# Attention, gated MLP and a spectral block on one core: row maxima for two heads at a time, more score buffers, one load for w_sg, a last product in fp16 halves, and the remaining tokens in two column groups

## The chip, the cores and the metric

The kernel runs on one core of a Trainium2 chip. The metric is the device time of one launch in microseconds (us), the median of several runs. A core has TensorE (PE in the profile, its weight loads PEld), VectorE (DVE), ScalarE (ACT), GpSimd (POOL) and SyncE (SP), which here only issues DMAs; ACT issues some as well. Each engine works through its own list of instructions in order, and waits on semaphores for the others.

## What is computed

Three blocks on a batch of 4 with 576 tokens, in float32; the outputs of one are the input of the next.

```python
def _attn_ref(q, k, v, w1, b1, w2):            # 4 batches, 8 heads, 576 tokens, 64 wide
    scores = scale * np.matmul(q, k.transpose(0, 1, 3, 2))
    ...
    h = np.maximum(x @ w1 + b1, 0.0)           # x: one number for each pair of positions
    bias = h @ w2
    scores = scores + bias.transpose(2, 0, 1)[None, :, :, :]
    scores = scores - np.max(scores, axis=-1, keepdims=True)
    attn = np.exp(scores)
    attn = attn / (np.sum(attn, axis=-1, keepdims=True) + 1e-09)
    return np.matmul(attn, v)

def _moe_ref(x, w_in, g_ln, w_sg, b_sg, w_out):
    h = gelu(x @ w_in)                         # tanh form
    u, v = (h[..., :512], h[..., 512:])
    v_n = (v - mu) / np.sqrt(var + 1e-06) * g_ln
    v_s = np.einsum('ts,bsd->btd', w_sg, v_n) + b_sg[None, :, None]
    return x + (u * v_s) @ w_out

def _moe2_ref(x, w_theta, w_tok_r, w_tok_i, w_ch):
    theta = x @ w_theta
    y = np.einsum('ts,bsd->btd', w_tok_r, x * cos(theta)) + np.einsum('ts,bsd->btd', w_tok_i, x * sin(theta))
    u = x + y
    return u + np.maximum(u @ w_ch, 0.0)
```

## The kernel before

**Tiling.** The 576 tokens are four tiles of 128 and one of 64. Heads go in pairs p (0 to 3) of a batch. Most products use fp16 halves: a float32 tile is scaled by a power of two and split into a high half and the rest, and three products (high·high, high·rest, rest·high) replace one. The final product with w_ch (`cp`) and that with w_out (`op`) split float32 into two tiles of TensorE's rounded float32 type instead.

**Order.** All operations are first recorded. A planner (`plan`, L433) then writes each engine's list, from a key of each operation, the tables `BIAS` and `SHIFT` (numbers for each group and for each kind of tile on each engine) and estimated costs (`cost`, L600). It also chooses the engine where the code offers several: a load may go to SP's or ACT's queue. Every instruction is emitted by one line, L417, so the profile's rows are told apart by the names of the tiles.

**Stages of the profiled execution.** To 80 us the bias of all heads is generated (tiles `pb`, `hq`, `bs`). From 80 to 190 us batch 0's attention runs, with w_in and w_sg being loaded and converted (`w1_load`, L806; raw tiles `rawwi`, `ws`). From 190 to 510 us attention of batches 1 to 3 runs mixed with the MLP of the batch before. From 510 to 650 us come batch 3's MLP, the products with w_out (`op`), conversion of the second block's weights, and the scales of its inputs. From 650 us on it is theta (`tp`), the token mix (`yp`) and the last product (`cp`).

**Attention.** `scores` (L865) fills PSUM tiles `s`, two heads at a time (128 tokens by 576). `att_tile` (L884) handles one head's tile: on DVE one pass adds the bias, writes `e`, and reduces the row's minimum into `m`; one more instruction adds a constant to the column `m`; ACT takes the exponential of `e` in place; ACT copies the high half into `p`, POOL subtracts for the low half; SP's queue issues a transposing DMA `pT`<-`p`; 14 matmuls `px` follow. Buffers: 3 of `e`, 4 of `m`, 6 of `p`, 7 of `pT`. The fifth token tile packs two heads' 64 rows (`pair_rem`, L920).

**The MLP.** `v_unit` (L1007) computes `vp`, x times the v half of w_in, for a token tile t: 12 matmuls of 512 columns out; then gelu, mean and variance (`st`, `mv`), the normalising factor (`nk`), and the two halves `n`, or `nr` for t = 4, where only 64 of the 128 partitions are used. `s_unit` (L1049) is the product with w_sg. Results pass through DRAM (`dg`, `dx`).

**The second block.** `conv_w` (L1142) loads and converts a weight tile, `put_w` (L1154) writes its two halves. `scale_of` (L1171) sums squares over partitions and makes a power of two by seven one-column instructions (`fs`, `fa`, `fb`, `fc`). `x_scale` (L1220) does so for each batch's input. `s4` (L1300) splits u into `sp_u` and computes `cp`; for each of four column blocks of a batch DVE takes the maximum with zero and adds u in one instruction (`bias<-cp,bias`: the output tile lies in old bias storage), and a DMA stores it.

## Time and profile before

| | |
|---|---|
| median of 3 runs | 831.53 us (829.93 to 832.4) |
| the profiled execution's own time | 833.19 us |
| its span, first to last instruction | 831.4 us |
| PE, share of the span busy | 88% (728.1 us) |
| PEld | 56% (465.0 us) |
| DVE | 73% (607.9 us) |
| ACT | 61% (507.0 us) |
| POOL | 41% (343.6 us) |
| DMA packets | 120.78 MB, mean 145 GB/s |
| mean granted TensorE clock | 0.926 |

The shares are means over stages with different limits, so the table of busy time by stretch is read first, then the chain of waits in each stretch (the chain goes back from the last instruction, at each step to what released it), and then single groups of instructions. In a row of groups the numbers behind x are the count, the busy time, the mean of one in ns, and the engine's idle time just before them with who ended it.

### The profile page before, as it was taken

What the parts mean: (1) busy time and instruction counts of PE and PEld (TensorE: products, weight loads), DVE (VectorE), ACT (ScalarE), POOL (GpSimd) and SP (SyncE); (2) the same over time, 40 slices, a digit from 0 to 9 for tenths busy, and PEclk for the clock granted to TensorE, in tenths of its full rate; (3) what the DMA queues carried; (4) which work ended last, traced back from release to release, by engine and by line L of the source; (5) the groups of instructions that cost most, each with busy time, mean ns of one, the idle gap of its engine ahead of it and who ended that gap; (6) DMA issues with size and microseconds to landing.
All of it is one profiled execution on the core that took longest, in us unless ns stands there. A gap on an engine that the chain in (4) does not pass through costs nothing.

```text
span 831.4 us, 17445 instructions
## 1 busy us (share of the span) xinstructions
PE 728.1 (88%) x6490; PEld 465.0 (56%) x6490; DVE 607.9 (73%) x1453; ACT 507.0 (61%) x953; POOL 343.6 (41%) x274
## 2 busy tenths in 40 slices
PE   5787368579889998989889988999889999999998
PEld 2233235256455554644545545776656677677887
DVE  6896388887887587975997989898988844572422
ACT  6896477666787676867747774565466642560500
POOL 0011334434666664756615662354246541360400
PEclk9998657578999998999978999999999999999999
DMA  6777959789998999889789777554452221030101
GB/s 196 193 181 155 261 133 216 166 160 190 188 188 191 169 205 182 160 180 213 195 212 199 157 157 203 172 157 164 117 120 54 40 53 56 1 80 29 44 15 58
DMA packets 221429, 120.78 MB, mean 145 GB/s; under 512 B 195360, under 2 KB 195744, under 8 KB 221344
## 3 DMA queue, kind: packets, MB, share of 16 engines
q1 hardware_dynamic: 211936, 98.86, 55.5%
q10 hardware_dynamic: 9408, 20.81, 7.9%
q8 instruction: 51, 0.84, 0.4%
q14 instruction: 34, 0.28, 0.1%
HBM read 47.68 MB, written 14.16 MB: 74 GB/s over the span
## 4 chain that ended last, share of the span: by engine, by line
PE 38%; DVE 15%; DMA 6%; issue 6%; ACT 3%; POOL 2%; ACTq 0%; DVEq 0%; POOLq 0%; SPq 0%
PE yp L417 11%; PE cp L417 6%; PE s L417 5%; DMA pT<-p 5%; PE sp L417 4%; PE px L417 3%; PE tp L417 3%; DVE bias L417 3%; PE up L417 3%; PE vp L417 2%; DVE e L417 2%; PE op L417 1%; DVE biasr L417 1%; DVE sp_g L417 1%; DVE gg L417 1%
## 5 line engine op out<-in xcount | busy, mean ns | idle before, releaser
L417 POOL TENSOR_TENSOR p<-e,p 128x576 f16<-128x576 f32 x144 | 190.3, 1332 | 240.8 <-ACT p L417 213.4
L417 PE MATMUL s<-kq 64*128 64x288 f32 (+1 forms) x640 | 153.3, 482 | 34.0 <-DVE m L417 32.3
L417 ACT ACTIVATE e<-e,m 128x576 f32<-128x576 f32 x144 | 110.5, 767 | 71.8 <-DVE m L417 51.9
L417 PEld LDWEIGHTS <-pT 128*128 128x128 f16 (+1 forms) x2240 | 84.2, 108 | 69.2 <-DMA pT<-p 32.5
L417 DVE CUSTOM_DVE_ANT_0 e<-s,bias 128x576 f32<-128x576 f32 x128 | 95.5, 750 | 35.8 <-PE s L417 29.9
L417 PE MATMUL px<-v,pT 128*128 128x64 f16 (+1 forms) x2240 | 95.5, 203 | 23.3 <-DMA pT<-p 19.2
L417 PEld LDWEIGHTS s<-kq 64*128 64x128 f32 (+1 forms) x640 | 70.5, 194 | 80.5 <-DVE m L417 46.7
L417 ACT ACTIVATE p<-e 128x576 f16<-128x576 f32 x144 | 94.7, 673 | 8.2 <-DMA pT<-p 3.3
L417 PEld LDWEIGHTS <-z 128*128 128x128 f16 x864 | 84.1, 98 | 25.5 <-ACT z L417 2.3
L417 PE MATMUL yp<-bias,z 128*128 128x288 f16 x576 | 76.5, 286 | 1.6 <-ACT z L417 1.6
L417 PE MATMUL pb<-hq,w2s 128*32 128x288 f32 x576 | 52.8, 430 | 17.1 <-ACT bs L417 8.1
L417 PE MATMUL op<-sp_g,wo 128*128 128x288 f32 x384 | 58.1, 307 | 7.6 <-ACT sp_g L417 2.8
L417 PE MATMUL vp<-wi,xT 128*128 128x512 f16 (+1 forms) x240 | 63.1, 400 | 0.7 <-DVE gg L417 0.5
L417 PEld LDWEIGHTS op<-sp_g,wo 128*128 128x128 f32 x384 | 53.6, 194 | 13.0 <-ACT sp_g L417 3.8
L417 PE MATMUL up<-xT,wi 128*128 128x64 f16 (+1 forms) x384 | 57.8, 290 | 0.0
L417 PE MATMUL sp<-ws,n 128*128 128x64 f16 (+1 forms) x384 | 56.9, 286 | 0.9 <-DVE gtu L417 0.7
L417 PE MATMUL cp<-sp_u,wc 128*128 128x288 f32 x384 | 54.0, 300 | 0.2 <-DVE bias L417 0.2
L417 PEld LDWEIGHTS cp<-sp_u,wc 128*128 128x128 f32 x384 | 51.8, 188 | 1.2 <-DVE bias L417 0.4
L417 DVE TENSOR_SCALAR hq<-lt,nl 128x576 f32<-128x576 f32 x96 | 45.7, 544 | 4.2 <-PE pb L417 2.3
L417 PEld LDWEIGHTS pb<-hq,w2s 128*32 128x32 f32 x576 | 20.8, 112 | 47.4 <-ACT bs L417 17.9
L417 PE MATMUL tp<-wt,xh 128*128 128x512 f16 x192 | 44.7, 380 | 1.9 <-DVE xh L417 1.9
L417 DVE SCALAR_TENSOR_TENSOR bias<-yp,iy,bias 128x576 f32<-128x576 f32 x16 | 13.0, 814 | 41.6 <-PE yp L417 41.5
(222 smaller groups left out, 1222.2 us busy)
## 6 DMA issues: line engine op xcount, KB each, us to landing
bias<-bs SPq DMA_DIRECT2D x32, 288.0 KB
kq<-kq SPq DMA_DIRECT2D x10, 576.0 KB
gr<-dg SPq DMA_DIRECT2D x15, 288.0 KB
out<-bias SPq DMA_DIRECT2D x15, 288.0 KB
xx<-dx SPq DMA_DIRECT2D x14, 288.0 KB
raw<-vp ACTq DMA_DIRECT2D x11, 320.0 KB
kq<-kq ACTq DMA_DIRECT2D x6, 576.0 KB
bias<-w_tok SPq DMA_DIRECT2D x6, 576.0 KB
```

Source lines behind the costliest of these rows:

```text
L417: getattr(getattr(self.nc, name), m)(*[res(x) for x in a], **out)
```

## The change

Six things are changed.

1. **Maxima of two heads.** A new `att_max` makes `e` for both heads of a token tile, with both minima in one two-column tile, and adds the constant once for both. `m` goes from 4 one-head buffers to 2 two-head ones, `e` from 3 buffers to 5, `p` from 6 to 5 and `pT` from 7 to 6.
2. **w_sg in one transfer**, where there were five.
3. **The remaining 64 tokens of `v_unit`**: each matmul of 64 rows by 512 becomes two of 64 by 256, into partitions 0 to 63 and 64 to 127, so that what follows works on 128 partitions by 256. Small copies move statistics between the partition halves, and `nr` is put together by two casts, a copy and two subtractions.
4. **The last product in scaled fp16 halves.** `wc` and the halves of u (`uh` instead of `sp_u`) are fp16, with power-of-two scales. w_ch's squares are summed in addition (four more ACT instructions), the scale of u comes from a bound, by the new `pow_of`. ACT now evicts `cp` with Relu and the inverse scale, and a DVE addition of u follows.
5. **Scales share one tile** `small`, of which each is a column.
6. **The planner**: the cost of 64-row outputs is halved, `SLACK` of ACT's loads is 0.456 instead of 0.038, and all numbers of `BIAS` and `SHIFT` are others.

```diff
 SHIFT = {
-    "@a0": 41.9784, "@a1": 58.4206, "@a10": -87.1642, "@a11": -56.0582, "@a12": -234.3945, "@a13": -112.4685,
...
+    "@a0": -222.2232, "@a1": 118.0225, "@a10": -218.6815, "@a11": 63.2763, "@a12": -170.5693, "@a13": -132.864,
...
+        late = U(SLACK if e == 2 else QUEUE) if op.dma and op.cost[i] > 0 else 0
...
-            self.ld(self.wsl[st], d["w_sg"][:, st])
+        self.ld(self.wsg[:, :5], d["w_sg"])
...
+    def att_max(self, b, p, t, tiles):
...
+        m = a.tile([P, 2, n], F32, tag=f"m{n}", bufs=2, name=f"m{b}_{p}_{t}")
...
+            s = a.tile([P, S], F32, tag="s", bufs=5, name=f"e{b}_{p}_{t}_{e}")
+            nc.vector.tensor_tensor_reduce(out=s.rearrange("p (n j) -> p n j", n=2), in0=ps[:, :, :SH],
+                                           in1=bias.rearrange("p (n j) -> p n j", n=2),
+                                           scale=-0.125, scalar=3e38, op0=ALU.add, op1=ALU.min,
+                                           accum_out=m[:, 0, e:e + 1])
...
+        nc.vector.tensor_scalar(m[:, 1], m[:, 0], LN2E, None, op0=ALU.add)
...
-        p16 = a.tile([P, 2, S], F16, tag="p16", bufs=6, name=f"p{u}")
+        p16 = a.tile([P, 2, S], F16, tag="p16", bufs=5, name=f"p{u}")
...
-        pT = a.tile([P, 9, P], F16, tag="pT", bufs=7, name=f"pT{u}")
+        pT = a.tile([P, 9, P], F16, tag="pT", bufs=6, name=f"pT{u}")
...
-                nc.tensor.matmul(ps[:m], self.xt_tok(b, cc, s, t), self.wi[:, w, cc, 512:DFF],
-                                 start=(cc == 0 and i == 0), stop=(cc == 3 and i == 2))
+                for h in range(P // m):
+                    nc.tensor.matmul(ps[h * m:h * m + m, :n], self.xt_tok(b, cc, s, t),
+                                     self.wi[:, w, cc, 512 + h * n:512 + h * n + n],
+                                     start=(cc == 0 and i == 0), stop=(cc == 3 and i == 2))
...
+        nc.vector.tensor_tensor(t, t, self.ck, op=ALU.mult)
+        u, w = self.pow_of(t, f"u{b}")
+        self.su[b] = u, w
...
-        sp = self.x_prep(b, self.p_sp2, "u", key - 10)
+            self.split16(x, self.x1[b][:, f], su)
...
+        nc.vector.tensor_tensor(ic, iu, self.ic, op=ALU.mult)
...
-            nc.vector.scalar_tensor_tensor(o.rearrange("p (n t) -> p n t", n=2), ps[:, :, :SH], 0.0,
-                                           self.x1[b][:, db].rearrange("p (n t) -> p n t", n=2),
-                                           op0=ALU.max, op1=ALU.add)
+            nc.scalar.activation(o.rearrange("p (n t) -> p n t", n=2), ps[:, :, :SH], AF.Relu, scale=ic)
+            self.tt(("vector", "gpsimd"), o, o, self.x1[b][:, db], ALU.add)
...
-        self.wc = self.p_s2.tile([P, 2, 4, DM], F32R, tag="wo", name="wc")
+        self.wc = self.p_s2.tile([P, 2, 4, DM], F16, name="wc")
+        sc, self.ic, _ = self.scale_of(self.ssq["w_ch"], "c")
```

The order is shown at three places. The first is ACT's list in batch 0's attention, where w_in's first two raw tiles are loaded; `p_0_1_2` stands for pair 0, head 1, token tile 2 (in `e_0_3_1` of the kernel after: pair 0, tile 3, head 1). Before:

```order
L417 ACTIVATE p_0_1_2_103<-e_0_1_2_1028 128x576
L417 DMA raw_1_1190<-vp 128x640
L417 DMA rawwi_0_1136<-w_in 128x1024
L417 DMA rawwi_1_1137<-w_in 128x1024
L417 ACTIVATE e_0_0_3_1107,sm_0_104<-e_0_0_3_1107,m_0_0_3_928 128x576
L417 ACTIVATE e_0_1_3_1144,sm_0_104<-e_0_1_3_1144,m_0_1_3_1080 128x576
L417 ACTIVATE p_0_0_3_791<-e_0_0_3_1107 128x576
L417 ACTIVATE p_0_1_3_925<-e_0_1_3_1144 128x576
L417 ACTIVATE v_1_114<-raw_1_1190,fc_v_207 128x2x320
```

After:

```order
L417 ACTIVATE p_0_0_3_728<-e_0_3_0_715 128x576
L417 ACTIVATE p_0_1_3_831<-e_0_3_1_809 128x576
L417 DMA raw_1_1174<-vp 128x640
L417 DMA rawwi_0_1130<-w_in 128x1024
L417 DMA rawwi_1_1131<-w_in 128x1024
L417 DMA ws<-w_sg 128x2880
L417 ACTIVATE e_0_4_0_878,sr_0_2_85<-e_0_4_0_878,m_0_4_87 128x576
L417 ACTIVATE e_1_4_0_1088,sr_1_2_86<-e_1_4_0_1088,m_1_4_88 128x576
L417 ACTIVATE p_0_2_0_902<-e_0_4_0_878 128x576
```

The loads of `rawwi` now stand behind the copies of `p` for token tile 3, and w_sg's single load has joined them on this list.

The second is SP's list at the start of batch 3's attention; here the first digit of a `pT` is the batch, then pair, head and tile, and `bias0<-w_out` and `bias0<-w_tok` are loads of raw weights for the second block. Before:

```order
L417 DMA bias0_78<-w_out 128x1024
L417 DMA dg_58<-gg1_2_5504 128x512
L417 DMA dx_57<-xT2_1_3939 128x1152
L417 DMA bias0_78<-w_tok 128x1152
L417 DMA dg_58<-gg1_3_5646 128x512
L417 DMA_TRANSPOSE pT3_0_1_2_5767<-p3_0_1_2_5433 128x9x128
L417 DMA dx_57<-xT2_2_5610 128x1152
L417 DMA bias0_78<-w_tok 128x1152
L417 DMA dx_57<-xT2_3_5614 128x1152
L417 DMA kq3_3_5883<-kq 128x1152
L417 DMA raw3_1_5932<-vp 128x640
L417 DMA_TRANSPOSE pT3_0_0_3_5962<-p3_0_0_3_5483 128x9x128
```

After:

```order
L417 DMA bias0_78<-w_out 128x1024
L417 DMA bias0_78<-w_tok 128x1152
L417 DMA dx_57<-xT2_1_3862 128x1152
L417 DMA_TRANSPOSE pT3_0_0_2_5630<-p3_0_0_2_5331 128x9x128
L417 DMA dx_57<-xT2_2_5549 128x1152
L417 DMA dg_58<-gg1_4_5637 512x1x64
L417 DMA dx_57<-xT2_3_5553 128x1152
L417 DMA bias0_78<-w_out 128x1024
L417 DMA kq3_3_5784<-kq 128x1152
L417 DMA raw3_1_5813<-vp 128x640
L417 DMA bias0_78<-w_tok 128x1152
L417 DMA_TRANSPOSE pT3_0_1_2_5842<-p3_0_1_2_5360 128x9x128
```

Before, ten loads stand around the transpose `pT3_0_1_2`, three of them raw weights. After, ten stand around `pT3_0_0_2` in these rows, four of them raw weights, and three more loads (one `bias0<-w_tok`, two `dg`) stand ahead of the first row, behind the transpose of `p3_0_1_1`: thirteen in all, five of raw weights, before `pT3_0_1_2` is issued.

The third is the end of the program. DVE's last rows before (`bias_78<-cp_0,bias_75` is maximum and sum of one column block):

```order
L417 SCALAR_TENSOR_TENSOR bias_75<-yp_2_10214,iy_123,bias_75 128x576
L417 TENSOR_TENSOR sp_u_10203<-bias_75,sp_u_10203 128x576
L417 SCALAR_TENSOR_TENSOR bias_75<-yp_3_10273,iy_123,bias_75 128x576
L417 TENSOR_TENSOR sp_u_10211<-bias_75,sp_u_10211 128x576
L417 SCALAR_TENSOR_TENSOR bias_78<-cp_0_10331,bias_75 128x576
L417 SCALAR_TENSOR_TENSOR bias_78<-cp_1_10389,bias_75 128x576
L417 SCALAR_TENSOR_TENSOR bias_78<-cp_2_10418,bias_75 128x576
L417 SCALAR_TENSOR_TENSOR bias_78<-cp_3_10444,bias_75 128x576
```

DVE after:

```order
L417 SCALAR_TENSOR_TENSOR bias_75<-yp_1_10173,small,bias_75 128x576
L417 SCALAR_TENSOR_TENSOR uh_3_10100<-bias_75,small,uh_3_10100 128x576
L417 SCALAR_TENSOR_TENSOR bias_75<-yp_2_10174,small,bias_75 128x576
L417 SCALAR_TENSOR_TENSOR uh_3_10163<-bias_75,small,uh_3_10163 128x576
L417 SCALAR_TENSOR_TENSOR bias_75<-yp_3_10236,small,bias_75 128x576
L417 SCALAR_TENSOR_TENSOR uh_3_10171<-bias_75,small,uh_3_10171 128x576
L417 TENSOR_TENSOR bias_78<-bias_78,bias_75 128x576 x4
```

ACT's last rows after, each `bias_78<-cp` being one eviction:

```order
L417 ACTIVATE uh_3_10091<-bias_75,small 128x576
L417 ACTIVATE uh_3_10100<-bias_75,small 128x576
L417 ACTIVATE uh_3_10163<-bias_75,small 128x576
L417 ACTIVATE uh_3_10171<-bias_75,small 128x576
L417 ACTIVATE bias_78<-cp_0_10294,small 128x576
L417 ACTIVATE bias_78<-cp_1_10352,small 128x576
L417 ACTIVATE bias_78<-cp_2_10383,small 128x576
L417 ACTIVATE bias_78<-cp_3_10408,small 128x576
```

The four evictions have gone from DVE to ACT, and DVE adds u to each behind them.

## Rows read from the trace of the kernel before

**Rows 1.** the page's chain of waits: share of the span by engine.

```profile
PE 38%; DVE 15%; DMA 6%; issue 6%; ACT 3%; POOL 2%; ACTq 0%; DVEq 0%; POOLq 0%; SPq 0%
```

**Rows 2.** busy time by stretch (columns in the first row), from batch 0's attention to the end.

```profile
core 0: us, PE busy (x) PEld busy (x) DVE busy (x) ACT busy (x) POOL busy (x), PEclk, DMA share, GB/s
80.00:190.00 110.00, 72.58 (x584) 43.70 (x580) 82.20 (x227) 73.54 (x156) 43.35 (x32) 0.62 0.82 184
190.00:300.00 110.00, 104.01 (x1144) 60.06 (x1143) 84.88 (x258) 82.50 (x168) 68.04 (x57) 0.99 0.95 187
...
405.00:510.00 105.00, 92.93 (x1035) 53.41 (x1034) 92.81 (x247) 66.86 (x132) 51.37 (x42) 0.90 0.83 189
510.00:650.00 140.00, 125.51 (x820) 87.26 (x819) 123.81 (x229) 81.98 (x149) 60.10 (x45) 0.99 0.47 133
650.00:831.40 181.40, 176.85 (x1315) 141.90 (x1312) 80.95 (x98) 64.49 (x103) 52.76 (x41) 1.00 0.13 39
```

**Rows 3.** chain from 650 us: its shares, then pieces (start, length, what).

```profile
by line: PE yp L417 50.4%; PE cp L417 28.1%; PE tp L417 11.9%; POOL z L417 2.0%; issue 1.5%; DVE bias L417 1.3%; DVE rr L417 1.2%; ACT rk L417 0.7%; DVE xh L417 0.4%; ACT xh L417 0.4%; ACT rr L417 0.4%; ACT z L417 0.4%; POOLq L417 0.0%
...
794.99 19.86 PE yp L417 x162
814.86 12.80 PE cp L417 x96
```

**Rows 4.** TensorE matmuls by shape (count, busy us, mean ns; idle before).

```profile
L417 PE MATMUL cp<-sp_u,wc 128*128 128x288 f32 x384 | 54.0, 300 | 0.2 <-DVE bias L417 0.2
```

**Rows 5.** timeline of the last 20 us (start, length, engine, operation).

```profile
815.74 0.69 ACT L417 ACTIVATE sp_u<-bias 128x576 fp32r<-128x576 f32 x1 [5.93 <-DVE bias L417]
...
827.68 0.76 DVE L417 SCALAR_TENSOR_TENSOR bias<-cp,bias 128x576 f32<-128x576 f32 x1 [2.44 <-PE cp L417]
```

**Rows 6.** ScalarE and VectorE groups by shape.

```profile
L417 ACT ACTIVATE bs<-pb,cb,rp 128x576 f32<-128x576 f32 x13 | 10.7, 823 | 3.9 <-DMA bias<-bs 2.3 <-PE pb L417 1.6
...
L417 DVE TENSOR_SCALAR m<-m 128x1 f32<-128x1 f32 x144 | 20.6, 146 | 1.1
...
L417 DVE TENSOR_TENSOR wc<-bias,wc 128x512 fp32r<-128x512 f32 x4 | 4.5, 1162 | 0.5 <-ACT wc L417 0.5
```

**Rows 7.** timeline of 86 to 98 us, ScalarE and its queue.

```profile
88.39 7.25 ACTq L417 DMA_DIRECT2D rawwi<-w_in  x2
...
95.75 0.77 ACT L417 ACTIVATE e<-e,m 128x576 f32<-128x576 f32 x1 [9.06 <-DMA rawwi<-w_in]
```

**Rows 8.** timeline pieces of TensorE: 64 columns wide, and bias generation's 32 columns.

```profile
12.37 2.15 PE L417 MATMUL pb<-hq,w2s 128*32 128x288 f32 x32
...
274.07 0.97 PE L417 MATMUL px<-v,pT 128*64 128x64 f16 x28
...
457.12 2.13 PE L417 MATMUL vp<-wi,xT 128*64 128x512 f16 x9
```

**Rows 9.** waits: who waited for whom (us in total, times, longest).

```profile
DVE e L417 <- POOL p L417: 7.2, 8, 1.9
```

**Rows 10.** SyncE's queue at batch 3's start.

```profile
396.80 4.08 SPq L417 DMA_TRANSPOSE pT<-p  x2
402.03 0.46 SPq L417 DMA_DIRECT2D bias<-w_out  x1
...
408.87 2.04 SPq L417 DMA_TRANSPOSE pT<-p  x1
411.31 0.32 SPq L417 DMA_DIRECT2D dx<-xT  x1
...
428.68 11.04 SPq L417 DMA_TRANSPOSE pT<-p  x6
```

**Rows 11.** chain in the same stretch.

```profile
417.17 16.56 issue
433.73 6.24 DMA pT<-p
```

**Rows 12.** VectorE's one-column arithmetic in a scale's chain.

```profile
L417 DVE TENSOR_SCALAR fa_x<-fa_x x8: 141/153/153, 579.3 to 644.5; 128x1 int32<-128x1 int32 x8
```

More of the change, by code (lines that the diff above doesn't have):

```diff
@@ L290 @@
-    "z": -223.7223, "zb": 1431.7686,
-}
-LOADF, LOADK = 9.424364169007852, 9.769672874286008e-139
-BV = -1.2289825808293022
[5 rows of a table added]
+    "@w_ch": 826.9009, "@w_out": 1276.3767, "@w_theta": -275.07, "@w_tok": 690.6464, "@y0": -945.0649,
[3 rows of a table added]
+    "fa_wi": 241.9602, "fa_ws": 866.725, "fac": -197.6344, "fb_v": 1268.1131, "fb_wi": -171.3458,
+    "fb_ws": -1066.8603, "fc_v": 939.5478, "fc_wi": -1431.7327, "fc_ws": 1172.4657, "fd_v": -453.2562,
+    "fd_wi": -530.3092, "fd_ws": 430.504, "fs": 0.2305, "fs_v": 808.5659, "fs_wi": 1806.8839,
@@ L462, in unlock @@
                 for i, e in enumerate(op.eix):
-                    heapq.heappush(wait[e], (op.ready + (U(SLACK) if op.dma and e == 2 else 0), op.skey, i, op))
+                    late = U(SLACK if e == 2 else QUEUE) if op.dma and op.cost[i] > 0 else 0
+                    heapq.heappush(wait[e], (op.ready + late, op.skey, i, op))
         def finish(op, stack):
@@ L882, in scores @@
         return tiles
-    def att_tile(self, b, p, kind, t, ps, sums, px):
+    def att_max(self, b, p, t, tiles):
+        nc, a = self.nc, self.p_att
+        n = len(tiles)
+        m = a.tile([P, 2, n], F32, tag=f"m{n}", bufs=2, name=f"m{b}_{p}_{t}")
+        es = []
+        for e, ps in enumerate(tiles):
+            bias = self.bm[t][:, 2 * p + e] if t < 4 else self.bm[4][:, p]
+            s = a.tile([P, S], F32, tag="s", bufs=5, name=f"e{b}_{p}_{t}_{e}")
[3 more added lines that the diff above has]
+                                           accum_out=m[:, 0, e:e + 1])
+            es.append(s)
+        nc.vector.tensor_scalar(m[:, 1], m[:, 0], LN2E, None, op0=ALU.add)
+        return [(s, m[:, 1, e:e + 1]) for e, s in enumerate(es)]
@@ L1174, in scale_of, with col, pow_of @@
         nc.tensor.matmul(ps[:, :n], self.ones, ss, start=True, stop=True)
-        t = self.const.tile([P, 1], F32, name=f"fs_{name}")
+        t = self.col("fs")
         nc.vector.tensor_reduce(t, ps[:, :n], mybir.AxisListType.X, ALU.add)
-        a, s, v = (self.const.tile([P, 1], I32, name=f"f{k}_{name}") for k in "abc")
+        return self.pow_of(t, name) + (t,)
+    def col(self, name):
+        self.cols += 1
+        return self.small[:, self.cols - 1:self.cols].named(name)
+    def pow_of(self, t, name):
+        nc = self.nc
+        a, s, v = (self.col("fa").bitcast(I32) for k in "abc")
         nc.vector.tensor_scalar(a, t.bitcast(I32), 23, None, op0=ALU.logical_shift_right)
@@ L1302, in s4 @@
         nc.grp = f"@z{b}"
-        sp = self.x_prep(b, self.p_sp2, "u", key - 10)
+        nc.key = key - 10
+        su, iu = self.su[b]
+        sp = []
+        for f in range(4):
+            x = self.p_sp2.tile([P, 2, S], F16, tag=f"uh{f}", name=f"uh{f}_{b}")
+            self.split16(x, self.x1[b][:, f], su)
+            sp.append(x)
+        ic = self.col("ic")
+        nc.vector.tensor_tensor(ic, iu, self.ic, op=ALU.mult)
         for db in range(4):
@@ L1332, in build @@
         self.wi = w.tile([P, 2, 4, DFF], F16, name="wi")
-        self.wsl = [w.tile([P, S], F32, name=f"ws{i}") for i in range(6)]
+        self.wsg = w.tile([P, 6, S], F32, name="ws")
+        self.wsl = [self.wsg[:, i] for i in range(6)]
         self.ws = [self.wsl[i - 1].bitcast(F16).rearrange("p (s j) -> p s j", s=2) for i in range(5)]
@@ L1340, in build @@
         self.p_c1 = nc.pool("c1p")
-        self.ssq = {"w_tok": self.sums(9, "k"), "w_theta": self.sums(4, "t")}
+        self.small, self.cols = self.const.tile([P, 80], F32, name="small"), 0
+        self.ssq = {"w_tok": self.sums(9, "k"), "w_theta": self.sums(4, "t"), "w_ch": self.sums(4, "c")}
         todo = [("w_out", DM, i) for i in range(4)] + [("w_theta", DM, i) for i in range(4)]
```

124 lines of the change are left out of this document (61 added, 63 removed), and 47 rows, old and new, of tables (BIAS, SHIFT).

## The prediction

> **What bounds the kernel now.** I read the page's chain of waits first. It names no single bound: PE holds 38% of the span, DVE 15%, DMA 6%, issue 6%, ACT only 3% [rows 1]. So I went to busy time by stretch [rows 2]. From 650 us on PE is busy 176.85 of 181.4 us and the DMA share is 0.13: the tail is bound by PE alone, and there a nanosecond off each matmul is a nanosecond off the end. From 510 to 650 us DVE is busy 123.81 of 140 us and DMA 0.47: that stretch hangs mostly on DVE. From 190 to 510 us everything is full at once: in 190 to 300 us PE has 104 of 110 us and DMA 0.95; in 405 to 510 us PE has 92.93 and DVE 92.81 of 105 us. From 80 to 190 us nothing is full (PE 72.58 of 110 us, at a granted clock of 0.62; DVE 82.20), so the time is in waits. What an edit is worth therefore depends on where it acts: in the tail it pays in full, in the mixed stretch a part, beside another bound nothing. The chain of the tail says the same: yp 50.4%, cp 28.1%, tp 11.9%, all PE [rows 3].
>
> My account starts from the profiled execution's own 833.19 us (span 831.4). It lies 1.66 us above the median 831.53, so I take 1.7 off at the end.
>
> **The last product in fp16 (tail).** The 384 cp matmuls [rows 4] move 128x288 each, as yp's do. At the end 96 of cp take 12.80 us, 133.3 ns each, and 162 of yp in fp16 halves take 19.86 us, 122.6 ns each [rows 3]. If fp16 cp runs at yp's pace, 384 x 10.7 ns = **-4.1 us**. The cp share of the tail's chain, 28.1% of 181 us = 51 us, is the same as 384 x 133.3 ns, so all of it is on the path. Bounds: 0 and -4.1; I take the latter since yp is the same shape and type.
>
> The eviction changes too. Now one DVE pass of 0.76 us ends the last block [rows 5]. After, ACT's Relu comes first, then DVE's sum, then the store. An ACT pass of this size takes 0.69 us from SBUF [rows 5] and 0.82 from PSUM [rows 6]. Only the last of 16 is exposed, since a block of 24 matmuls (3 us) covers each of the others: **+0.8 us**, between +0.7 and +0.9. The splits of u keep one ACT and one DVE pass each, so they are nil; if ACT came late there, PE would wait, but ACT is busy only 64.49 of 181.4 us [rows 2].
>
> **The stall on w_in's load (batch 0).** ACT's queue issues two loads of raw w_in at 88.39 us and is held 7.25 us; the next exponential starts at 95.75 after 9.06 us of idleness, which the profile puts on that load [rows 7]. The changed order has the two loads behind token tile 3's copies, and w_sg's single load behind them. The nine operations that follow can still be held, and the conversion of raw w_in comes earlier in the list than before, so part of the wait may come back as a wait for the data. Bounds 0 and -7.3; **-3 us**, rather less than half, because in this stretch DVE and ACT have slack to catch up and only px and pT wait behind.
>
> **Remaining tokens in column groups.** Before, 64-column vp matmuls run at 2.13/9 = 237 ns [rows 8], so 48 of them are 11.4 us. After, twice as many of half the length: if two groups run at once half is saved, -5.7 us, and if not 0. That groups of columns do run at once is seen in bias generation: 32 matmuls of 32 columns by 288 take 2.15 us, 67 ns each, against 122.6 ns for one full yp of the same length [rows 3, 8]. Batch 3's quarter lies under DVE from 510 us on, so 4.3 us remain where PE is 89 to 95% busy but shares the bound; I take **-2 us**. The DVE passes on 128x256 instead of 64x512 gain about what the added copies of statistics cost; nil, and DVE covers it in all stretches but the one from 510 us.
>
> The extra weight loads could eat this: 96 instead of 48. In the trace 28 px matmuls of 64 columns, each with a weight load of its own, take 0.97 us, 35 ns for load and product together [rows 8]. A load hides behind the 237/2 ns of the product before it. The Trainium skill, "TensorEngine Tiling (Array Packing)", Restrictions, says that column tiling turns the fast weight load off, and "TensorE: Matmul & The Clock Gate", LDWEIGHTS, gives columns/1.2 ns for a plain load, so an estimate of 53 ns for 64 columns. If none were hidden, 96 x 53 ns = 5.1 us would cancel nearly all of the saving, and the forecast would stand at 823 instead of 821. The row of px, 35 ns, speaks against a cost of that size.
>
> **Maxima of two heads.** The one-column m takes 146 ns, 144 times [rows 6]. 80 remain: 64 x 0.146 = 9.3 us less on DVE, all of it in 80 to 510 us. DVE is 75 to 88% busy there and is not alone on the path: **-2 us**, about the fifth that DVE has of the chain [rows 1]. Against it stands a new wait: the first head's exponential starts only when the second head's `e` and the common m are done, 0.75 us later. ACT holds 3% of the chain, 25 us; were all of that exponentials at 0.77 us, 32, half of them first heads, this costs 16 x 0.8 = +13 us at the far end. The added buffers of e let DVE go on meanwhile, so I take none of it. Bounds -9.3 and +13.
>
> **Buffers.** Five of e instead of three take away DVE's wait for p, 7.2 us in 8 waits [rows 9]: 0 to -7.2; some of these turn into waits for PE's scores, **-2 us**. One buffer less of p and of pT shortens the run-up in front of SP's queue. A transpose takes 11.04/6 = 1.84 us [rows 10]; one at each of three batch boundaries is 5.5 us, of which chain gaps show some: **+1.5 us**, between 0 and +5.5.
>
> **Small scales and weights.** Four batches get seven one-column steps and two more (36), w_ch eight, one for w_tok's sum: 45 x 0.153 us [rows 12] = +6.9 us on DVE in or after its own stretch. On the other side the four DVE splits of wc, 1.162 us each [rows 6], now stand behind the first yp of batch 0, in PE's tail, where DVE is 45% busy: -4.6. The scales of u and w_ch are wanted only by cp, so some of the 45 fall there too. **0**, bounds -4.6 and +6.9.
>
> **Moved order.** Tables move rows on all engines. Where I can price it, it is the fourth case below; otherwise 0.
>
> Sum: -4.1 + 0.8 - 3 - 2 - 2 - 2 + 1.5 + 0 = **-10.8 us**; 833.2 - 10.8 = 822.4; less 1.7, **821 us**.
>
> **Rivals.**
>
> A, the forecast: 821, with its own range 812 to 829.
>
> B, only the tail pays. In the mixed stretch DMA is at 0.95 and four engines are near full; what DVE or PE saves becomes waiting for transposes. For it: DMA share, and the chain's 6% of DMA and 6% issue [rows 1, 2]. Against it: PE's 104 of 110 us. -4.1 + 0.8 = -3.3: 833.2 - 3.3 - 1.7 = **828**, spread 825 to 833.
>
> C, attention gives what its waits offer. Each attention term at about twice my value, the shorter buffers at no cost: -3.3 - 6 - 4 - 4 - 4 - 1.5 (of the scales) = -22.8, so **809**. For it: DVE, ACT and PE are all relieved together. Against it: these savings overlap in time.
>
> D, slower: SP's queue at batch 3's start. There SP issues loads in order, and a transpose behind them waits. Between 400.9 us (end of two transposes) and 428.68 (start of six) ten loads and one transpose of 2.04 us pass [rows 10], 25.7 us of loads, 2.6 each; and PE's chain shows 16.56 us of issue and 6.24 us of pT just there [rows 11]. The new order has thirteen loads before the second transpose, five of raw weights instead of three. Three more at 2.6 us are +7.7; at the pace of the second five ((428.68 - 410.91)/5 = 3.55) +10.7. On its own on top of B it gives 828 + 8 to 11, so **837** (with A's gains it would be 830). It decides from a hole over about 3 us, if the attention terms give nothing. For it: PE did wait in the same place. Against it: PE can work on MLP 2 meanwhile, and loads moved here are missing elsewhere.
>
> That the kernel does not do what it says I rule out for m, w_sg, cp and the column groups, whose rows are in the lists.
>
> **How the numbers follow.** A 0.48 (0.47 faster, 0.01 within), B 0.20 (0.09 faster, 0.11 within, because 0.3%, about what a measurement here can tell from no change, puts the border at 829.0), C 0.13 (faster), D 0.19 (slower). Together: faster 0.69, same 0.12, slower 0.19. For the range I leave out a part of C (below 806, 0.05) and the upper half of D (above 836, 0.10), and so take 806 to 836; the bounds of m's wait and of the scales (+13, +6.9) lie in D's tail.
>
> **What would show it.** Right: cp at 123 ns each in the tail; the last Relu at 0.7 to 0.8 us ahead of a DVE sum; no idleness over 3 us of ACT near 90 us; 64-column vp pairs at about 120 ns a matmul; DVE's m group at 80; DVE's wait for p near nothing; batch 3's start with no hole in PE. Wrong: cp still at 133 ns; a hole of PE over 10 us near 400 to 440 us (D); the stretch from 190 to 510 us as long as before with less DVE work in it (B); ACT's waits for m well above 0.8 us each.

## The result, and the profile after

The changed kernel takes 836.15 us in the median of 20 runs, the kernel before 829.94 us in 20 runs beside them: a ratio of 1.0057, with an interval from 1.0032 to 1.0082. So it is slower by 0.6%; I had forecast 821 us and a gain. (Some executions are disturbed and several per cent longer; ratios leave them out, so they can differ a little from the quotient of two medians.) The profiled execution took 836.54 us, about its median; its span is 834.7 us, 3.3 more than before. That of the kernel before, 833.19 us, lies 3.3 us above the 829.94, so the two traces compared below show only a part of the loss.

Several terms came out as predicted. The last pieces of the changed kernel's chain of waits (start, length, what) answer to [rows 3, 5]:

```profile
798.22 20.00 PE yp L417 x162
818.23 11.77 PE cp L417 x96
...
830.03 0.75 ACT bias L417
...
830.80 0.76 DVE bias L417
```

96 of cp take 11.77 us, 122.6 ns each instead of 133.3, and the Relu adds 0.75 us. The 64-column vp matmuls answer to [rows 8]; this is the timeline of PE:

```profile
553.70 1.50 PE L417 MATMUL vp<-wi,xT 128*64 128x256 f16 x24
```

24 in 1.50 us are 62.5 ns each. The 12 they replace took 12 x 237 = 2.84 us, so 1.34 us are saved in a batch, 5.4 in four: the pairs of column groups do run at once, and their extra weight loads are hidden (of the 5.1 us that the prediction weighed for them nothing shows). By the page's groups these matmuls are 6.9 us busy instead of 12.6. And the stall of [rows 7] is gone from ACT; in the changed kernel's timeline it issues the load and goes on:

```profile
92.52 0.53 ACTq L417 DMA_DIRECT2D rawwi<-w_in  x1
...
95.36 0.77 ACT L417 ACTIVATE e<-e,m 128x576 f32<-128x576 f32 x1 [2.13 <-DVE m L417]
```

The busy time by stretch (columns as in [rows 2]) shows where PE's gain and the added work lie:

```profile
190.00:300.00 110.00, 96.78 (x992) 54.69 (x992) 81.05 (x215) 75.46 (x158) 63.80 (x54) 0.97 0.88 176
...
405.00:510.00 105.00, 88.02 (x897) 51.23 (x896) 92.78 (x227) 63.40 (x128) 48.97 (x40) 0.92 0.86 168
510.00:650.00 140.00, 130.73 (x1017) 92.95 (x1018) 124.65 (x277) 85.68 (x162) 63.82 (x48) 0.99 0.54 150
650.00:834.70 184.70, 178.38 (x1358) 132.09 (x1355) 89.16 (x123) 81.13 (x126) 55.13 (x43) 1.00 0.17 44
```

From 190 to 300 us PE is busy 96.78 us instead of 104.01, with the DMA share down from 0.95 to 0.88: no engine is fuller, all have more holes. (By the marks below, this stretch also ends at an earlier point of the work than before.) One wait stands out in the list of waits of the changed kernel (us in total, times, longest); the same row of before had 3.3 us in 3 waits, and the second answers to [rows 9]:

```profile
ACT p L417 <- DMA pT<-p: 22.9, 9, 7.2
...
DVE e L417 <- POOL p L417: 5.0, 4, 2.2
```

ACT, which copies e into p, now waits 22.9 us for a transpose to give a buffer of p free.

For a comparison by stage I marked the same events in every trace: the last eviction of bias generation (bs), the start of DVE's score pass number 18, 36, 72, 108 and 126 of 144 (36 to a batch, so s36 opens batch 1 and s108 batch 3), DVE's last gg (in batch 3's MLP), DVE's first pass over yp, and the end. Each mark is the start of that instruction. Times in us; the labels below the second line are those of the experiments.

| trace | bs | s18 | s36 | s72 | s108 | s126 | gg | yp | end |
|---|---|---|---|---|---|---|---|---|---|
| before | 81.7 | 133.7 | 195.4 | 283.2 | 379.9 | 443.2 | 593.4 | 656.2 | 831.4 |
| after | 87.4 | 123.5 | 193.2 | 288.9 | 384.0 | 452.2 | 603.9 | 663.0 | 834.7 |
| a0_kept | 88.8 | 124.9 | 192.1 | 287.2 | 382.0 | 447.8 | 598.2 | 657.3 | 829.1 |
| a1_m_one_col | 89.0 | 125.1 | 192.1 | 284.9 | 380.2 | 446.3 | 597.6 | 655.6 | 827.4 |
| c4_m_one_col_again | 87.3 | 136.3 | 200.1 | 292.7 | 389.4 | 456.0 | 606.0 | 664.2 | 836.0 |
| d1_ws_later | 87.3 | 128.5 | 196.0 | 289.6 | 388.4 | 454.3 | 605.5 | 663.0 | 834.8 |
| c3_before_buf_556 | 80.6 | 132.0 | 196.2 | 282.7 | 386.7 | 459.4 | 607.1 | 669.9 | 845.1 |
| e2_before_457 | 81.5 | 132.9 | 197.3 | 282.3 | 380.3 | 450.4 | 599.0 | 661.9 | 837.3 |
| e3_before_466 | 81.0 | 129.0 | 192.8 | 279.5 | 376.3 | 445.7 | 594.6 | 657.3 | 832.5 |
| e1_cp_alone | 82.0 | 131.2 | 192.7 | 280.0 | 377.4 | 441.5 | 593.1 | 656.5 | 831.7 |

Read as the lag of after behind before: +5.7 at bs, -10.2 at s18, -2.2 at s36, +5.7 at s72, +4.1 at s108, +9.0 at s126, +10.5 at gg, +6.8 at yp, +3.3 at the end. The removed stall leads by 10 us, and 8 us of it are gone 70 us later; two stretches lose more (s36 to s72 and s108 to s126), and from gg on 7 come back. So the loss lies in the attention from batch 1 to the middle of batch 3: from s36 to s126 the ten traces of the changed order with its own buffers (those in the table, and a2, b1, c1, d2, d3 below) take 4.6 to 13.5 us more than before, while from s126 to the end they take 4.8 to 9.2 us less. One trace is one execution: a1 and c4 are the same program and end 8.6 us apart, so stage lengths count here where several traces agree. Nor is each trace the middle of its runs: those of a0, c3 and e3 show the fastest execution of each.

### The profile page after: what moved, and what is told of

Read it like the earlier page. It is cut to its first block, busy times and chain, and to the rows that moved or that the text cites. A ratio compares the mean times of both kernels' runs of the same rounds, so it can differ in the third digit from the quotient of the medians.

```text
span 834.7 us, 17494 instructions
## 1 busy us (share of the span) xinstructions
PE 722.5 (87%) x6540; PEld 456.1 (55%) x6540; DVE 612.3 (73%) x1445; ACT 518.7 (62%) x986; POOL 339.2 (41%) x274
## 5 line engine op out<-in xcount | busy, mean ns | idle before, releaser
L417 POOL TENSOR_TENSOR p<-e,p 128x576 f16<-128x576 f32 x144 | 187.7, 1317 | 255.8 <-ACT p L417 214.8
L417 PE MATMUL s<-kq 64*128 64x288 f32 (+1 forms) x640 | 157.9, 497 | 40.2 <-DVE m L417 39.9
L417 ACT ACTIVATE e<-e,m 128x576 f32<-128x576 f32 x144 | 110.0, 765 | 54.1 <-DVE m L417 47.6
L417 PEld LDWEIGHTS <-pT 128*128 128x128 f16 (+1 forms) x2240 | 87.2, 110 | 72.4 <-issue 36.5
L417 PE MATMUL px<-v,pT 128*128 128x64 f16 (+1 forms) x2240 | 98.8, 206 | 24.9 <-DMA pT<-p 15.8
L417 PEld LDWEIGHTS s<-kq 64*128 64x128 f32 (+1 forms) x640 | 73.5, 200 | 84.3 <-DVE m L417 55.5
L417 ACT ACTIVATE p<-e 128x576 f16<-128x576 f32 x144 | 92.8, 671 | 24.4 <-DMA pT<-p 22.9
L417 PE MATMUL pb<-hq,w2s 128*32 128x288 f32 x576 | 51.1, 450 | 19.4 <-ACT bs L417 13.5
L417 PE MATMUL vp<-wi,xT 128*128 128x512 f16 (+1 forms) x288 | 55.0, 348 | 2.3 <-DVE xT L417 1.2
L417 PE MATMUL cp<-uh,wc 128*128 128x288 f16 x384 | 49.0, 286 | 0.4 <-ACT bias L417 0.4
L417 POOL TENSOR_TENSOR z<-rk,z 128x512 f16<-128x512 f32 x18 | 22.7, 1267 | 55.5 <-ACT z L417 55.5
L417 PEld LDWEIGHTS <-wc 128*128 128x128 f16 x384 | 37.6, 98 | 11.0 <-issue 0.5
```

The costliest lines, as they stand in the source:

```text
L417: getattr(getattr(self.nc, name), m)(*[res(x) for x in a], **out)
```

## The experiments

There were three suspects: the pair of maxima, by a wait of DVE; the later end of bias generation; and SP's queue with the shorter buffers. A fourth, the load of w_sg, came from the first runs. Each run below takes one of them out or puts one into the kernel before. The planner would put a changed program in another order, so in nearly all kernels below the order that it found is written in as a list, and an edit moves only the rows that it names. First the changed kernel with its own order written in, to see that this alone changes nothing:

```diff
+ORDER = (...)   # every engine's rows as in the changed kernel
```

> The changed kernel with the planner's order written into it as a table, for comparison with the next three, which change one thing each in that order. All theories: the changed kernel's own time, 0.3 to 0.8% above the kernel before; the last evictions of bias generation near 87 us.

Measured: 1.010 (1.0031 to 1.0169), which contains the ratio of the changed kernel, and the same marks within 6 us.

**The pair of maxima.** Two one-column instructions in the place of the common one, everything else kept:

```diff
-nc.vector.tensor_scalar(m[:, 1], m[:, 0], LN2E, None, op0=ALU.add)
+for e in range(n):
+    nc.vector.tensor_scalar(m[:, 1, e:e + 1], m[:, 0, e:e + 1], LN2E, None, op0=ALU.add)
```

> The changed kernel in its own order, but the constant is added to the two maxima by two one-column instructions side by side instead of one of two columns. Theory of the shared port (the two-column form waits while GpSimd works, 344 ns on average and up to 1.23 us): each one-column instruction takes about 146 ns and none over 0.2 us, DVE's time for them falls from 24 to 21 us, and the kernel gains 2 to 5 us. Rival (m is off the path, the loss is in buffers and order): the groups shrink in the same way and the time stays within 1 us.

> The changed kernel in its own order with one-column maxima once more, for comparison on the same chip as the three others. Theory of the shared port: 2 to 5 us under the changed kernel's 836 to 839, near 832.6. Rival (the first time was chance): 835 to 838.

Measured: 1.0047 (1.0006 to 1.0088) and, of the same program again, 1.0044 (1.0005 to 1.0082). The times can't tell it from 1.0057. The rows can. Here is tile m on DVE in before (first and second line: m and, for later, the reciprocal r of a batch's sums), with minimum, median and maximum in ns:

```profile
L417 DVE TENSOR_SCALAR m<-m x144: 96/146/155, 37.4 to 497.9; 128x1 f32<-128x1 f32 x144
L417 DVE TENSOR_SCALAR r<-sm x16: 152/168/587, 97.4 to 499.5; 128x8 f32<-128x8 f32 x16
```

the same in the changed kernel:

```profile
L417 DVE TENSOR_SCALAR m<-m x80: 132/163/1234, 31.9 to 505.4; 128x2 f32<-128x2 f32 x64, 128x1 f32<-128x1 f32 x16
```

and in a1_m_one_col:

```profile
L635 DVE TENSOR_SCALAR m<-m x144: 94/144/155, 33.3 to 499.0; 128x1 f32<-128x1 f32 x144
```

80 instructions take 24.3 us where 144 took 21.0 (sums of the single rows), since 17 of the 64 with two columns last over 250 ns, up to 1234. All 17 began while GpSimd was at a tensor operation and ended 24 to 29 ns after it. One of the longest, in the changed kernel's timeline:

```profile
200.54 2.52 POOL L417 TENSOR_TENSOR p<-e,p 128x576 f16<-128x576 f32 x2 [0.86 <-ACT p L417]
200.66 1.19 DVE L417 TENSOR_SCALAR m<-m 128x2 f32<-128x2 f32 x1
201.94 0.78 ACT L417 ACTIVATE e<-e,m 128x576 f32<-128x576 f32 x1 [0.90 <-DVE m L417]
```

The two-column m takes DVE 1.19 us beside GpSimd's first subtraction for p, and ACT behind it waits 0.90. Of before's 144 one-column instructions 78 began inside a GpSimd operation, 67 of them ended inside it too, and none was longer than 155 ns; nor was one of a1's, where 44 began inside. So the wider instruction waits for GpSimd and the narrow one doesn't. The Trainium skill, "SBUF — State Buffer", "Who interferes with whom", has an exclusive lock of a port pair that VectorE shares with GpSimd, for VectorE instructions in a two-port mode, which it says tensor_scalar can enter: the loser is blocked until the other is done. The 24 to 29 ns agree with that; whether these instructions are in such a mode no run shows. In batch 1 the five traces with the pair (after, a0, a2, d1, d3) lose 7.1 us to before in the mean, the four without (a1, c4, c1, d2) 5.1. That would make the wait's price some 2 us there, but the two groups overlap (5.8 to 7.9 and 4.8 to 6.0), and the times show no gain of that size; the other 5 have another cause.

**Bias generation.** The changed order has five more bs evictions on ACT, and its last eviction is 5.7 us later. In a2 they are back on DVE; in c2 the kernel before gets ACT's; in c1 the changed kernel (with the one-column m) has all of before's bias generation. The first, as rows of DVE:

```diff
 TENSOR_SCALAR hq<-lt,nl 128x576
+TENSOR_SCALAR bs<-pb,rp,cb 128x576
 TENSOR_SCALAR hq<-lt,nl 128x576
```

> The changed kernel in its own order, but five evictions of bias generation go back from ScalarE to VectorE, as in the kernel before. Theory of bias generation (ScalarE became its bound): the last eviction comes 4 to 6 us earlier, near 82 us, and the kernel gains 2 to 5 us. Rival (batch 0's attention waits for something later anyway, such as the loads of w_in): the last eviction comes earlier and the time stays within 1 us.

> The kernel before in its own order, with five of VectorE's eleven evictions of bias generation on ScalarE, as in the changed kernel. Theory of bias generation: its last eviction comes 3 to 6 us later and the time rises by 2 to 6 us over the kernel before. Rival (hidden): the last eviction is later and the time stays within 2 us.

> The changed kernel in its own order with one-column maxima, and the operations of bias generation in the order and on the engines of the kernel before, at the places that they hold in the changed order. Theory of bias generation: its last eviction comes 4 to 7 us earlier (near 82 us instead of 88) and the time falls by 2 to 6 us from that of one-column maxima alone (832.6), to the kernel before or under it. Rival (batch 0's attention takes it back): the last eviction is early and the time within 2 us of 832.6.

Measured: a2 1.0216 (1.0148 to 1.0284), c2 1.0042 (0.999 to 1.0095), c1 1.007 (1.0034 to 1.0105). a2 doesn't do what it was meant for, since its last eviction is no earlier (88.9 us); why it is slower still was not looked into, beyond a wait of ACT for w_in's data (6.5 us) like that of c4 below. c2 is the clean one: the same evictions on ACT move bs by 0.9 us, and the trace stays within 2 us of before's to the end. Nor does before's bias generation gain anything in c1 (bs 85.9 us, end 833.5). So where the evictions run is not the cause; why bias generation ends later in all of the changed orders stays open.

**SP's queue.** My fourth rival had the transposes behind loads on SP's queue. In b1 (with the one-column m) the transposes stand ahead of the loads around them on SP's list; one piece of it:

```diff
-DMA kq<-kq 128x1152
-DMA rawwi<-w_in 128x1024
 DMA_TRANSPOSE pT<-p 128x9x128
-DMA rawwi<-w_in 128x1024
 DMA_TRANSPOSE pT<-p 128x9x128
 DMA_TRANSPOSE pT<-p 128x9x128
+DMA kq<-kq 128x1152
+DMA rawwi<-w_in 128x1024
 DMA_TRANSPOSE pT<-p 128x9x128
+DMA rawwi<-w_in 128x1024
```

> The changed kernel in its own order with one-column maxima, and on SyncE's list alone every transpose moved ahead to the place behind the GpSimd subtraction that feeds it, as far as free buffers allow; the loads it passes come later. Theory of SyncE's queue (transposes wait behind loads that wait themselves): PE's wait for the transposes falls and the time falls by 3 to 8 us against the kernel with one-column maxima (832.6). Rival (transposes wait for p and for free buffers, not for the queue): within 2 us.

Measured: 1.019 (1.0135 to 1.0246), slower. The place in the list alone is no remedy (a transpose that stands first and waits for its p holds the loads, which would explain the loss, but no run shows it apart). Nor does this edit shorten the hole of [rows 10] at batch 3's start: from 412.95 us, the end of a transpose, to 445.73, less one transpose of 1.97, loads hold SP for 30.8 us, against 28.2 in a1. So what fell is the remedy; whether that hole costs time, b1 does not test.

**The buffers, in the changed order.** Other shares of the room: 3, 6, 7 of e, p and pT as before; and, with the one-column m, 4, 5, 7 and 4, 6, 6. Where the list asked for more buffers than there are, rows were moved behind what frees one. b3 is b2 with transposes at batch 3's start ahead of the loads.

```diff
-s = a.tile([P, S], F32, tag="s", bufs=5, ...)
+s = a.tile([P, S], F32, tag="s", bufs=3, ...)
-p16 = a.tile([P, 2, S], F16, tag="p16", bufs=5, ...)
+p16 = a.tile([P, 2, S], F16, tag="p16", bufs=6, ...)
-pT = a.tile([P, 9, P], F16, tag="pT", bufs=6, ...)
+pT = a.tile([P, 9, P], F16, tag="pT", bufs=7, ...)
```

> The changed kernel in its own order as far as dependences allow, but with the buffers of the kernel before: 3 of e, 6 of p, 7 of pT instead of 5, 5, 6. Theory of the shorter p and pT: ScalarE's wait for the transposes before it writes p falls from 22.9 us to under 10 and the kernel gains 2 to 6 us. Rival (5 of e are worth what they took): the waits for e come back and the kernel is slower by 2 to 10 us.

> As the kernel with one-column maxima, with 4 buffers of e, 5 of p, 7 of pT instead of 5, 5, 6. Theory that the seventh pT is worth more than the fifth e: 2 to 5 us faster than 832.6. Rival (the order is made for five e): slower by 5 to 30 us, as 3, 6, 7 was by 90.

> As the kernel before it in this list (4, 5, 7), and three transposes at the start of batch 3 moved ahead of the loads of weights on SyncE's list, which seven pT allow. Theory of the hole at batch 3's start: transposes of the third and fourth tile start 10 us and more earlier there, and the time is 2 to 8 us less than with 4, 5, 7 alone. Rival (PE has MLP work there, the hole costs nothing): within 2 us of it.

> As the kernel with one-column maxima, with 4 buffers of e, 6 of p, 6 of pT instead of 5, 5, 6. Theory that the sixth p is worth more than the fifth e: ScalarE's wait for transposes ahead of p falls from about 20 us to under 8, and the time is 2 to 5 us under 832.6. Rival (the order is made for five e): slower by 5 to 30 us.

Measured: 1.1216 (1.1143 to 1.1289), 1.0459 (1.0403 to 1.0515), 1.0371 (1.0318 to 1.0424) and 1.0349 (1.0297 to 1.0402). The changed order is made for five of e, and gives 12% away with three; so nothing about the price of one p or one pT can be read from these four. b3 is 8 us faster than b2 (medians 859.0 and 867.0 of six runs each, intervals nearly apart), as the theory of the hole had it. Its trace ends no earlier, but shows the slowest of b3's executions beside the fastest of b2's.

**The buffers, in the order of before.** The clean form: the kernel before, its order written in, and three numbers changed. Where a buffer is missing, rows move behind what frees it: in the traces none on DVE, one on GpSimd, no more than two transposes on SP, and some copies of p and loads on ACT. c2 above, with its order written in too, shows no loss that is clear of noise.

```diff
-tag="s", bufs=3    -tag="p16", bufs=6    -tag="pT", bufs=7
+tag="s", bufs=5    +tag="p16", bufs=5    +tag="pT", bufs=6
```

> The kernel before in its own order, with the changed kernel's buffers: 5 of e, 5 of p, 6 of pT. Theory of the shorter p and pT: ScalarE's wait for the transposes ahead of p grows from 3 us to over 10 and the time rises by 3 to 10 us. Theory of the prediction (five e gain 2, the shorter ones lose 1.5): within 2 us. Rival (five e are worth more): 2 to 7 us faster.

> The kernel before in its own order with 4 buffers of e, 5 of p, 7 of pT. If the shorter p is what costs in 5, 5, 6 (ScalarE holds up before it writes p): 8 to 19 us slower than the kernel before, and ScalarE's wait for transposes over 15 us. If it is pT: within 3 us.

> The kernel before in its own order with 4 buffers of e, 6 of p, 6 of pT. If the shorter pT is what costs (transposes wait for the products that free it, behind them SyncE's queue): 8 to 19 us slower than the kernel before. If it is p: within 3 us.

Measured: 5, 5, 6 gives 1.0226 (1.0176 to 1.0275); 4, 5, 7, one p less, 1.0162 (1.0115 to 1.0209); 4, 6, 6, one pT less, 1.016 (1.0101 to 1.0219). The last two are less sure than their intervals say: the medians of all runs, 841.43 and 844.39 beside 834.58 us, make 0.8% and 1.2%. In the table c3 is level with before up to s72 (-0.5) and then loses 7.3 us in batch 2 and 9.4 us from s108 to s126; e2 and e3 lose 6.8 and 6.1 us in that last stretch. The waits of c3_before_buf_556 name the buffer:

```profile
PEld L635 <- DMA pT<-p: 37.2, 25, 4.3
ACT p L635 <- DMA pT<-p: 27.4, 14, 6.3
```

those of e2_before_457

```profile
ACT p L635 <- DMA pT<-p: 28.0, 11, 5.6
```

and those of e3_before_466

```profile
ACT p L635 <- DMA pT<-p: 15.2, 4, 5.5
```

against 3.3 us in 3 waits before. With fewer p, ACT stands at its copy until a transpose has read the old one; the transpose stands on SP behind loads; and behind ACT's copy stand its next exponentials. Of the stretch from s108 to s126 these waits are 11.4, 11.0 and 9.7 us in c3, e2 and e3, 2.6 before. SP's list there is nearly the same, but it stands longer: the hole of [rows 10] grows from 25.7 us to 31.4, 27.4 and 31.7, and behind it the next load, of v, opens a second one. SP's queue before (the six transposes of [rows 10] ahead of it end at 439.72) and in c3_before_buf_556:

```profile
440.78 0.33 SPq L417 DMA_DIRECT2D raw<-vp  x1
441.21 19.58 SPq L417 DMA_TRANSPOSE pT<-p  x9
```

```profile
438.55 12.24 SPq L635 DMA_TRANSPOSE pT<-p  x7
459.16 0.33 SPq L635 DMA_DIRECT2D raw<-vp  x1
459.60 1.32 SPq L635 DMA_TRANSPOSE pT<-p  x1
```

From transpose to transpose it is 1.5 us before and 8.8, 8.7 and 7.5 us in the three; SP waits there for DVE and for an earlier load of v. In the same stretch PE stands idle 18.2, 16.3 and 15.1 us instead of 8.1, which covers the loss. Less of either kind is enough for a loss of 0.8 to 1.6%, both of them cost 2.3%. That the length of the holes is the cause is read from this and from b3; no run takes the holes away in the order of before.

**The load of w_sg.** Before, the five slices of w_sg came one by one. The changed kernel has one load of all, right behind the two of raw w_in. My theory after the first runs was that it takes their bandwidth. In d1 it stands behind the second conversion of w_in, in d2 so too with the one-column m, in d3 ahead of the loads of w_in (as rows of ACT's queue):

```diff
+DMA ws<-w_sg 128x2880
 DMA rawwi<-w_in 128x1024
 DMA rawwi<-w_in 128x1024
-DMA ws<-w_sg 128x2880
```

> The changed kernel in its own order, with one row of ScalarE's list moved: the load of w_sg is issued behind the second conversion of w_in (about 7 us later) instead of right behind w_in's loads. Theory of the collision: w_in's conversion begins 5 to 7 us after the issue of its load, the six transposes before it take 17 to 19 us, the third pair's first score tile comes at 122 to 126 us, and the median falls by 3 to 7 us from 836 to 839. Rival (the collision is with other traffic): the median stays within 2 us.

> As d1, with one-column maxima. Theory of the collision and of the shared port together: 1 to 3 us less than d1, 828 to 832, at or under the kernel before. Rival (the port is off the path): as d1 within 1 us.

> The changed kernel in its own order, with one row of ScalarE's list moved: the load of w_sg is issued ahead of w_in's two loads. Theory of the collision: w_in's conversion begins 12 us or more after the issue in every execution, the third pair's first score tile comes at 134 us or later, and the median rises by 3 to 8 us to 841 to 846. Rival: within 2 us of 836 to 839.

Measured: 1.0003 (0.9963 to 1.0042), 1.0026 (0.9983 to 1.0069) and 1.0018 (0.9977 to 1.0059). All three are level with before and a little under the changed kernel, whose interval theirs overlap; but the place that should have been bad (d3) does as well as the good one. The kernel before, too, was slower beside these three (median 833.5 us of 29 runs) than beside the changed kernel (829.9), and their own medians, 834.0, 837.0 and 833.6 us, are no better than the 832.6 of a1. The theory isn't borne out. What the load of w_in does is seen better in two executions of one program. ACT, its queue and SP's in a1_m_one_col:

```profile
91.15 17.02 SPq L635 DMA_TRANSPOSE pT<-p  x6
...
94.58 0.57 ACTq L635 DMA_DIRECT2D rawwi<-w_in  x1
...
100.43 1.20 ACT L635 ACTIVATE ri<-rawwi 128x512 f32<-128x512 f32 x2
```

and in c4_m_one_col_again:

```profile
89.53 24.98 SPq L635 DMA_TRANSPOSE pT<-p  x6
...
91.73 0.45 ACTq L635 DMA_DIRECT2D rawwi<-w_in  x1
...
105.25 0.66 ACT L635 ACTIVATE ri<-rawwi 128x512 f32<-128x512 f32 x1 [6.89 <-DMA rawwi<-w_in]
```

From issue to the conversion it is 5.9 us in one and 13.5 us in the other, and ACT waits 6.89 us for the data. Score pass 18 comes 11.2 us later, the end 8.6. The stall that the change removes from the issue comes back, in some executions, as late data; in the trace of the changed kernel itself it does not (6.2 us from issue to conversion).

**The last product alone.** The kernel before with the fp16 last product only; its order is the same up to about 545 us and the planner's own behind that:

```diff
-sp = self.x_prep(b, self.p_sp2, "u", key - 10)
+self.split16(x, self.x1[b][:, f], su)
...
-nc.vector.scalar_tensor_tensor(o, ps, 0.0, x1, op0=ALU.max, op1=ALU.add)
+nc.scalar.activation(o, ps, AF.Relu, scale=ic)
+self.tt(("vector", "gpsimd"), o, o, x1, ALU.add)
```

> The kernel before with the fp16 last product alone (scales, halves of u, Relu on ScalarE, sum on VectorE); maxima, buffers, w_sg and the column groups as before, and the same order up to about 545 us. Theory of the parts (the tail's gain is real, the attention's changes eat it): 3 to 5 us less from the first yp to the end, the attention stages as before, the time 3 to 6 us under the kernel before. Rival (the small scales' arithmetic costs VectorE what the tail gains): within 2 us.

Measured: 1.0049 (1.0009 to 1.0088), no gain (the medians of all runs, 836.45 beside 834.58 us, make 0.2%). cp runs at its 122.6 ns, and yet from the first yp to the end it is 175.2 us as before. PE is busy with cp 48.7 us there instead of 54.0; but the new order leaves nine more matmuls of theta to this stretch (`tp`, 27.1 us instead of 25.2), and PE stands idle 6.1 us in it instead of 4.6. The chain of waits leaves PE at one place:

```profile
by line: PE yp L419 51.8%; PE cp L419 23.6%; POOL z L419 5.5%; ACT rk L419 2.9%; ACT z L419 2.5%; DVE bias L419 2.2%; ACT bias L419 2.1%; ACT rr L419 2.0%; issue 2.0%; DVE rr L419 1.1%; ACTq L419 0.0%
...
771.30 1.16 POOL z L419
...
772.49 1.61 POOL z L419
...
781.90 0.73 ACT bias L419
782.63 0.04 issue
782.67 5.18 PE cp L419 x41
```

(The shares are of the stretch from 760 us on; the pieces are start, length, what.) From 770.6 to 782.7 us the chain goes over theta's range reduction on ACT, DVE and GpSimd and an eviction. PE is not idle meanwhile (busy 11.75 of 12.1 us with yp and cp); it waits 0.35 us for the eviction. So the run shows that a gain on cp can be lost to the order of the rest; it does not show that cp is off the path.

## Why the prediction was wrong, point by point

**Where the sum failed.** The terms of the attention (stall, column groups, maxima, e, p and pT) came to -7.5 us; at s126 the changed kernel is 9.0 us late. Behind s126 the sum had -3.3 us, and 5.7 are measured.

**The buffers, the step that failed and could be measured.** The sum had +1.5 us for one p and one pT less, "between 0 and +5.5", from one transpose of 1.84 us at each batch boundary, and -2 for the five of e. In before's order the three numbers cost 13.7 us of the trace and 2.3% of the time. The price of a buffer was taken from the length of a transpose; what ACT waited for is the transpose and all that stands ahead of it on SP's queue. [rows 10] showed the place: a hole of 25.7 us of loads at batch 3's start. In the changed kernel's SP queue the same place reads:

```profile
398.55 5.64 SPq L417 DMA_TRANSPOSE pT<-p  x2
...
418.60 1.84 SPq L417 DMA_TRANSPOSE pT<-p  x1
...
435.60 7.62 SPq L417 DMA_TRANSPOSE pT<-p  x4
```

From 404.2 to 435.6 us, less one transpose, it is 29.6 us. So rival D had a place that got worse, with +3.9 us instead of its +7.7 to +10.7; in the stretch from s108 to s126 ACT waits 13.0 us for transposes to free p, much as in c3, e2 and e3, and the stretch is 4.9 us longer. But D's sign, a hole of PE over 10 us from 400 to 440 us, is not there (the longest is 1.6 us; PE is idle 10.3 us in the whole stretch, 8.1 before), and that its 837 us lies beside the measured 836 is luck. D and the buffers look like one mechanism, which I had priced as two. How much of the changed kernel's 0.6% is the buffers' can't be said: its order was planned for them, and no order planned for 3, 6, 7 with all else changed was measured. The stages agree only in part: c3 loses in batch 2 and from s108 to s126, the changed kernel in batch 1 and from s108 to s126. The moved order, which the sum had at 0 without a price, is in all of the changed kernels and was never taken out; it is the rival that stays open.

**The maxima.** Forecast 9.3 us less on DVE, -2 us of the time, against a possible wait of ACT. Measured +3.3 us on DVE, by the wait for GpSimd; the feared wait of ACT for m did not grow (47.6 us in all, 51.9 before). The row that says so stood in before's trace and wasn't read: r, an operation of the same kind, 128x8 wide, with a maximum of 587 ns and a median of 168, where the one-column m has a maximum of 155. Four of its 16 are long (239 to 587 ns), and each ended 26 or 27 ns after a GpSimd subtraction. I took the price of a wider form from the narrower one's row.

**The stall on w_in.** Gone, as the forecast said, and 10.2 us ahead at s18; I counted 3. Most of the lead is lost by s36. DVE, not ACT, is the engine nearest to full there. Of before:

```profile
99.30:133.70 34.40, 24.56 (x174) 14.50 (x174) 29.29 (x74) 26.21 (x58) 15.05 (x11) 0.54 0.73 163
133.70:195.40 61.70, 44.34 (x411) 28.25 (x412) 51.55 (x154) 40.10 (x82) 24.95 (x19) 0.67 0.88 175
```

and after:

```profile
94.40:123.50 29.10, 22.77 (x152) 13.21 (x152) 22.00 (x57) 21.55 (x51) 9.72 (x8) 0.55 0.94 248
123.50:193.20 69.70, 51.86 (x442) 33.41 (x442) 59.16 (x165) 41.50 (x85) 25.11 (x19) 0.61 0.83 161
```

The third busy time is DVE's. From pass 9 to s18 (the first row of each) it does 7.3 us less in the changed kernel, from s18 to s36 7.6 us more, and in the second stretch it is 84% busy before and 85% after (51.55 of 61.7, 59.16 of 69.7). So the stall had covered work of DVE that now comes later. (That DVE bounds the stretch is read from its share and from PE's waits for m, 14.4 us there; no run tests it.) My reason for taking less than half of it, that "DVE and ACT have slack to catch up", was the wrong way round for DVE. The second part of the step, that the wait may come back as a wait for the data, is what c4 shows.

**The last product.** 10.7 ns off each of 384 and +0.75 us for the Relu are right, and in the changed order the -3.3 us came: from the first yp to the end it is 171.8 us instead of 175.2, and 171.8 or 171.9 in all ten traces of that order with its own buffers. In e1, in another order, nothing came. That "all of it is on the path" was thus true of one order and not a property of the product. A chain made of PE alone shows that PE was last everywhere; not by how much the others were ahead.

**Column groups, scales, e.** The groups' -5.4 us on PE is the bound; that any of it reached the end isn't seen, in a stretch where PE fell from 104.01 to 96.78 us without getting shorter. DVE's wait for p went from 7.2 to 5.0 us, not to nothing; its wait for scores, which I had expected to grow, fell from 35.2 to 22.4. The move of wc's splits into the tail, entered as 0 with a bound of -4.6, fits the stretch from gg to yp, 59.1 us instead of 62.8; no run has it, or the scales, apart.

**The rivals.** B, that the middle gives nothing, was nearest in kind: its sum of 828 lacked the losses of 195 to 290 and 380 to 452 us. The chance of slower was 0.19, for one mechanism at one place; the table shows two stretches that lose, and a later start.

**Open.** Some 5 us of batch 1 (s36 to s72) that neither the pair of maxima nor the load explains: DVE's and PE's busy times there differ by 2.1 and 0.9 us, so it lies in waits (PE is idle 13.0 us there instead of 6.0). The buffers don't explain it either: with them, c3 is 1.4 us faster than before in that batch. The 5.7 us of bias generation. And what decides in which execution w_in's load lands late. No kernel here is shown to be faster than the one before.

## What to carry to other kernels

A tile's buffer is worth more than the transfer that frees it takes, since what stands ahead in the queue is waited for too: look at the longest hole between two transfers of its kind before giving one away. Where the next engine in a mixed stretch is as full as DVE here (85%), a removed stall may only show how much of its work the stall had hidden: add its busy time up to the next mark, and take the gain from that sum. Before an instruction is made wider, look at the maximum, not the median, of the rows of that wider form.
